# Another listed order for the engines of an attention-plus-MLP kernel: all that stands behind the first GEMM 1 product

## The chip, the cores and the metric

The kernel runs on one core of one Trainium2 chip. The metric is the device time of one execution in microseconds (us), lower is better. A core has a matrix engine (TensorE, PE in the profile, with its weight loads as PEld), a vector engine (VectorE, DVE), a scalar engine (ScalarE, ACT), a general engine (GpSimd, POOL) and a fifth one that only issues transfers (SyncE, SP). Each engine works through its own list of instructions in order; between engines there are semaphores.

## The reference

```python
# q, k, v: [4, 8, 768, 64] float32 (batch, head, position, width)
k_sum = k.reshape(B, H, nb, 32, D).max(axis=3)        # 24 blocks of 32 keys
v_sum = v.reshape(B, H, nb, 32, D).mean(axis=3)
scores_l = where(|i - j| < 16, scale * q @ k.T, -1e9)  # a narrow band
scores_s = scale * q @ k_sum.T + log(32)
a = softmax(concat([scores_l, scores_s]))
attn = a @ concat([v, v_sum])
x = attn as [3072, 512]
h = x @ w_in                                           # w_in [512, 2048]
out = (h * clip(h + 3, 0, 6) / 6) @ w_out              # w_out [2048, 512], out [3072, 512] float32
```

## The kernel before

The 3072 rows of x are worked on as eight tiles of 384 rows, two for each of the four batches. For every tile s there are 16 products of GEMM 1, named `F{s}x{ft}` (ft is the column block of 128 of w_in): four matmuls of 128x384 each, then `relu` on ACT (line 671) and `gate` on DVE (line 672), which together make the activation and write one slice of the buffer g. GEMM 2 is `G{s}{ts}x{a}`: three row groups ts for a tile, each with four parts of four matmuls of 128x512 (line 684); the last row group of the last tile is cut into pieces of 256, 128 and 128 columns (`G71x0`, `G71x256`, `G71x384`). A copy (`.4`) brings the sum from PSUM to a buffer `ot`, and a store (`.5`) writes it out.

Attention comes ahead of each pair of tiles. `K`, `Q`, `V`, `H` are loads of keys, queries and values, `w` the turning of keys and queries on DVE and ACT with the block maxima, `s` scores (small matmuls, then `exp` on ACT and masking on DVE), `u` the sums of values, `v` the products with the values (for the first four tiles with transposes `v....3` on PE), `h` copies of borders. `I0`, `I2`, `I4`, `I8`, `I12` load w_in: I0 its column blocks 0 and 1, I2 blocks 2 and 3, I4 blocks 4 to 7, I8 blocks 8 to 11, I12 blocks 12 to 15. `O0` to `O3` load w_out. All these loads are issued by POOL on one queue.

What sets the order on every engine is a table of names, `ORDER`. Each step of the kernel is recorded first with its engine, its inputs and the buffers that it touches (`Plan.op`), and `Plan.issue` then walks through the table and issues the steps in just that order. A name may end in `:A` or `:D`, which puts a copy on ACT or on DVE. Where a step needs a buffer out of a pool, it takes the one that has been free for longest, so another order also gives other buffers. The pools have three PSUM banks `h` and one `o`, two pairs of banks `S`, and four buffers `ot`.

```python
for n, token in enumerate(ORDER.split()):
    ...
    key, _, e = token.partition(":")
    o = named.pop(key)
    ...
        b.pool, b.slot = min(((p, s) for p in b.among for s in self.pools[p]), key=lambda x: since[id(x[1])])
    ...
    (partial(o.fn, {"A": "ACT", "D": "DVE", "P": "POOL"}[e]) if e else o.fn)()
```

A product of GEMM 1 waits for its own load of w_in, since it names the column block among its inputs, and the load names the blocks that it writes:

```python
op("POOL", "dma1024", lambda: nc.gpsimd.dma_start(out=w_in_sb[:, :, lo * 128:hi * 128], in_=w_in_v[:, :, lo * 128:hi * 128]),
   w=[("win", ft) for ft in range(lo, hi)], size=128 * (hi - lo))
...
op("PE", f"F{hi - lo}", lambda lo=lo, hi=hi: mms(lo, hi), r=[xt[s], ("win", ft)] + (xs if len(parts) == 1 else xs[lo:hi]), w=[h])
```

The first five products of tile 0 are issued as four separate steps (`F0x3.0` to `F0x3.3`) because x of that tile arrives in four pieces.

Of the kernel before, what the change touches and what calls it, by code (L numbers as in the profile page):

```python
# [15 lines left out]
D = 64  # L16
# [21 lines left out]
s001.2 F0x8.0 F0x8.1 F0x8.2 F0x5.1 I0.0 F0x5.2 F0x11.0 F0x1.0 F0x11.1 F0x11.2 F0x1.1 F0x1.2 F0x1.3 F0x1.4 F0x1.5 v410.0 v410.1  # L38
F0x7.0 F0x7.1 F0x7.2 v410.2 F0x10.0 F0x10.1 I12.0 F0x13.0 F0x13.1 F0x15.0 F0x15.1 F0x13.2 F0x10.2 v411.3 v411.4:D v410.3
v410.4:A F0x15.2 F0x14.0 F0x14.1 F0x14.2 F0x9.0 F0x9.1 F0x9.2 F0x0.0 F0x0.1 F0x2.0 F0x2.1 K13.0 K10.0 c.12:A F0x0.2 K12.0 K11.0  # L40
w10.0 Q1w1.0 F1x14.0 F1x14.1 F1x14.2 F1x4.0 F1x4.1 F1x4.2 F1x2.0 F1x2.1 F1x2.2 w10.1:D F0x2.2 F0x2.3 F0x2.4 F0x12.0 F0x12.1
F0x12.2 F1x8.0 F1x8.1 F1x8.2 F1x1.0 F1x1.1 F1x1.2 F0x0.3 F0x0.4 F0x0.5 F0x2.5 F1x9.0 F1x9.1 F1x9.2 F1x5.0 F1x5.1 F1x5.2 F1x15.0
F1x15.1 w11.0 w11.2 F1x15.2 w11.3:D Q1w4.0 Q1w2.0 Q1w0.0 w10.2 w10.3:D q6.0 q6.1:A q7.0 q7.1:A F1x7.0 F1x7.1 w11.1:A F1x7.2
F1x12.0 F1x12.1 F1x12.2 O0.0 G02x0.0 Q1w5.0 Q1w3.0 q4.0 q4.1:A q5.0 q5.1:A F1x6.0 F1x6.1 F1x6.2 O1.0 G02x0.1 s100.0 s100.1
s100.3 F1x3.0 w12.0 F1x11.0 F1x11.1 w13.0 w13.2 F1x3.1 F1x11.2 w12.2 w12.1:D O2.0 G02x0.2 s101.0 s101.1 O3.0 F1x10.0 G02x0.3
G02x0.4:A w13.3:D w13.1:A s101.3 F1x0.0 G00x0.0 G00x0.1 w12.3:D s100.2 s101.2 s100.4 V10.0 h100.0:D F1x10.1 h110.0:A F1x10.2
F1x3.2 s110.0 s110.1 s110.2 s101.4 s110.3 G00x0.2 G00x0.3 G00x0.4:A V12.0 u4.0 h130.0:D h120.0:A F1x0.1 u4.1:D u4.2:A u4.4:D
u4.3:D u4.5:D G02x0.5 G01x0.0 G01x0.1 G01x0.2 s110.4 F1x0.2 h111.0:A v100.0 v100.1 v100.2 h121.0:A v101.0 v101.1 v101.2 G01x0.3
G01x0.4:A K20.0 K21.0 K22.0 K30.0 K23.0 w21.0 F1x13.0 F1x13.1 F1x13.2 v100.3 v100.4:A w20.0 w21.3 G12x0.0 w21.2:A v101.3
v101.4:A V22.0 H2.0 h101.0:A w20.3 G12x0.1 G12x0.2 F2x2.0 F2x2.1 F2x11.0 F2x2.2 F2x11.1 F2x11.2 s111.0 w23.0 s111.3 F2x1.0  # L50
# [30 lines left out]
F7x6.2 G51x0.5 F7x8.0 F7x8.1 F7x8.2 G62x0.0 F7x4.0 F7x4.1 F7x4.2 F7x3.1 F7x3.2 F7x2.0 G62x0.1 F7x15.0 F7x2.1 F7x2.2 F7x15.1
F7x15.2 F7x0.0 G62x0.2 F7x0.1 G62x0.3 F7x7.0 F7x7.1 F7x0.2 G71x0.0 G62x0.4:D G62x0.5 F7x7.2 F7x11.0 F7x11.1 G61x0.0 F7x11.2
F7x14.0 G71x0.1 G71x0.2 G71x256.0 G61x0.1 F7x14.1 F7x14.2 G71x0.3 G71x0.4:A G72x0.0 G72x0.1 G71x0.5 G41x0.5 G70x0.0 G61x0.2
G61x0.3 G61x0.4:A G52x0.5 G70x0.1 G70x0.2 G72x0.2 G50x0.0 G50x0.1 G61x0.5 G50x0.2 G50x0.3 G72x0.3 G70x0.3 G50x0.4:A G50x0.5
G70x0.4:D G70x0.5 G60x0.0 G60x0.1 G60x0.2 G72x0.4:D G72x0.5 G60x0.3 G71x256.1 G71x256.2 G60x0.4:D G60x0.5 G71x256.3 G71x256.4
G71x384.0 G71x384.1 G71x384.2 G71x384.3 G71x384.4:D G71x384.5
"""


# [720 lines left out]
```

## Time and profile before

| | before |
|---|---|
| time, median of 3 runs | 217.0 us (216.62 to 217.43) |
| span of the profiled execution | 214.9 us |
| PE busy | 208.8 us (97%) |
| DVE busy | 162.7 us (76%) |
| ACT busy | 135.9 us (63%) |
| POOL busy | 49.5 us (23%) |

The profiled execution is shown by its span alone, from the first to the last instruction. The median is 2.1 us above that span, and this is taken as what lies around it. PE is close to always busy, so a microsecond in which PE has nothing to do is, from the first product of GEMM 1 on, a microsecond of the whole. Busy time of a matmul counts its passage through the array, so that matmuls overlap; the pace is read from the start of one group to the start of the next.

### The profile page before, as it was taken

The numbers are of one execution on the slowest core, as the hardware profiler recorded it, in microseconds if no ns is written. First come the engines' busy times: TensorE is split into PE (matmuls) and PEld (weight loads), VectorE is DVE, ScalarE is ACT, GpSimd is POOL, SyncE is SP. The second block draws the span as 40 slices with busy tenths as digits, with TensorE's granted clock in tenths as the row PEclk, the third lists the DMA queues.
The fourth block names the chain that finished last, engine by engine and source line by source line (L and its number), as shares of the span: only waits on it lengthen the run. The fifth ranks groups of instructions, "written<-read, shape, count | busy, mean of one in ns | idle before, by whom it ended". The sixth has DMA issues, their size and how long they took to land.

```text
span 214.9 us, 6125 instructions
## 1 busy us (share of the span) xinstructions
PE 208.8 (97%) x2564; PEld 119.7 (56%) x2564; DVE 162.7 (76%) x318; ACT 135.9 (63%) x264; POOL 49.5 (23%) x66
## 2 busy tenths in 40 slices
PE   7998999999999999999999999999999999999994
PEld 7566656555555565565555555555555555564443
DVE  6987999999899999898899889887865555550021
ACT  3987878887898988756578696566346355520110
POOL 7977358906643244000000000000000000000000
PEclk9999999999999999999999999999999999999999
DMA  5999999999999999930334234113314400113123
GB/s 75 159 155 189 203 188 170 190 203 162 206 160 187 181 135 151 108 146 11 38 37 143 28 37 110 49 21 39 70 19 81 78 0 3 49 49 122 52 80 139
DMA packets 91724, 22.68 MB, mean 106 GB/s; under 512 B 82224, under 2 KB 88752, under 8 KB 91696
## 3 DMA queue, kind: packets, MB, share of 16 engines
q0 software_dynamic: 62288, 14.41, 72.7%
q1 hardware_dynamic: 29264, 7.80, 15.4%
q8 instruction: 20, 0.33, 0.6%
q10 hardware_dynamic: 144, 0.07, 0.1%
q14 instruction: 8, 0.07, 0.1%
HBM read 28.82 MB, written 6.29 MB: 163 GB/s over the span
## 4 chain that ended last, share of the span: by engine, by line
PE 86%; POOL 5%; DMA 4%; DVE 1%; ACT 1%; issue 1%; POOLq 0%
PE h L667 38%; PE o L684 33%; PE h L684 5%; DMA qwide<-in_q_dram 4%; PE S L624 3%; PE S L513 3%; POOL vaug L344 2%; PE S L554 1%; ACT vaug L242 1%; POOL first L306 1%; PE S L637 1%; POOL qwide L326 1%; PE S L440 1%; PE S L667 1%; POOL first L313 1%; PE h L582 1%
## 5 line engine op out<-in xcount | busy, mean ns | idle before, releaser
L667 PE MATMUL h<-x,win 128*128 128x384 bf16 x500 | 91.1, 326 | 0.3 <-DVE g L672 0.3
L671 ACT ACTIVATE r<-h 128x384 f32<-128x384 f32 x125 | 58.7, 492 | 38.8 <-PE h L667 36.8
L672 DVE SCALAR_TENSOR_TENSOR g<-r,h 128x384 bf16<-128x384 f32 x125 | 65.7, 546 | 22.7 <-ACT r L671 20.1
L684 PE MATMUL o<-wout,g 128*128 128x512 bf16 x336 | 81.7, 379 | 0.0
L667 PEld LDWEIGHTS <-win 128*128 128x128 bf16 x512 | 48.7, 98 | 35.9 <-issue 0.5
L684 PEld LDWEIGHTS <-g 128*128 128x128 bf16 x416 | 38.7, 98 | 37.4 <-issue 0.3
L521 ACT ACTIVATE at<-S 120x768 bf16<-120x768 f32 x24 | 18.6, 811 | 5.5 <-PE S L513 5.4
L242 ACT COPY ot<-o 128x512 f32<-128x512 f32 x17 | 10.0, 586 | 15.4 <-PE o L684 14.2
L522 DVE TENSOR_TENSOR at<-at,mask 96x768 bf16<-96x768 bf16 x24 | 12.6, 549 | 2.0 <-ACT at L521 1.6
L606 DVE TENSOR_TENSOR xn<-S,rc 128x768 bf16<-128x768 f32 x14 | 13.3, 950 | 0.3
L242 DVE COPY ot<-h 128x512 f32<-128x512 f32 (+1 forms) x3 | 1.6, 555 | 14.3 <-PE h L684 14.3
L344 POOL DMA_DIRECT2D vaug<-in_v_dram x10 | 11.8, 1191 | 0.4 <-DMA first<-in_k_dram 0.2
L684 PE MATMUL h<-wout,g 128*128 128x128 bf16 (+2 forms) x80 | 11.4, 294 | 0.0
L468 DVE TENSOR_REDUCE red<-kaug 128x24 bf16<-128x768 bf16 x12 | 11.2, 942 | 0.1
L242 ACT COPY vaug<-vaug 32x640 bf16<-32x640 bf16 (+3 forms) x17 | 8.9, 574 | 0.8 <-DMA vaug<-in_v_dram 0.5
L242 ACT COPY vaug<-vs 24x1536 bf16<-24x1536 bf16 x6 | 8.8, 1468 | 0.6 <-DVE vs L242 0.5
L456 DVE STREAM_TRANSPOSE kaug<-kraw 128x768 bf16<-128x768 bf16 x8 | 8.1, 1020 | 0.3 <-PE S L513 0.3
L778 PE MATMUL o<-idle 128*128 128x64 bf16 (+2 forms) x70 | 7.0, 278 | 1.1 <-DVE idle L288 1.1
L334 POOL DMA_DIRECT2D kraw<-in_k_dram x8 | 5.9, 737 | 8.9 <-DVE kaug L456 7.3
L513 PEld LDWEIGHTS <-kaug 32*128 32x128 bf16 x576 | 5.3, 92 | 4.4 <-issue 3.6
L643 DVE STREAM_TRANSPOSE y<-xn 128x768 bf16<-128x768 bf16 x8 | 7.6, 964 | 0.2
L624 PEld LDWEIGHTS <-at 120*64 120x64 bf16 x336 | 6.2, 111 | 2.6 <-issue 1.5
(107 smaller groups left out, 183.6 us busy)
## 6 DMA issues: line engine op xcount, KB each, us to landing
out_dram<-ot SPq DMA_DIRECT2D x19, 256.0 KB, 2.3
vaug<-in_v_dram POOLq DMA_DIRECT2D x6, 384.0 KB, 13.1
wout<-in_moe_w_out_dram POOLq DMA_DIRECT2D x4, 512.0 KB, 9.9
win<-in_moe_w_in_dram POOLq DMA_DIRECT2D x3, 512.0 KB, 10.8
kraw<-in_k_dram POOLq DMA_DIRECT2D x8, 192.0 KB, 12.9
x<-y SPq DMA_DIRECT2D x64, 24.0 KB, 2.0
first<-in_k_dram POOLq DMA_DIRECT2D x6, 192.0 KB, 12.3
first<-in_q_dram POOLq DMA_DIRECT2D x6, 192.0 KB, 12.3
```

Source lines behind the costliest of these rows:

```text
L242: {"ACT": nc.scalar.copy, "DVE": nc.vector.tensor_copy, "POOL": nc.gpsimd.tensor_copy}[eng](o, i)
L344: op("POOL", "dma128", lambda: nc.gpsimd.dma_start(out=o[BLK:WIN, a:z, 0:D], in_=rows[:, a:z]), w=[("v", b % 2, c) for c in range(lo, hi)] ...
L468: op("DVE", "max", lambda: nc.vector.tensor_reduce(red.slot[:], w[:, :, BLK:WIN].rearrange("p t (n c) -> p t n c", n=2), axis=AX.X, op=ALU ...
L513: nc.tensor.matmul(X[g // 2].slot[:, g % 2, i * QB:(i + 1) * QB], kaug[2 * u + m][rows, t], qT[rows, 2 * u + m, t * QB:(t + 1) * QB], star ...
L521: op("ACT", "exp", lambda a=a, e=e: nc.scalar.activation(a, X[e].slot[0:KEYS, :, 0:HALF], AF.Exp, scale=scl), r=[X[e]], w=[("at", p, half)])
L522: op("DVE", "masking", lambda m=m: nc.vector.tensor_tensor(m, m, mask[:, low(half):low(half) + HQ].unsqueeze(1).to_broadcast([WIN, 2, HQ, ...
L606: nc.vector.tensor_tensor(o, src[..., 0:D], r.unsqueeze(len(r.shape)).to_broadcast(list(o.shape)), op=ALU.mult)
L624: nc.tensor.matmul(X.slot[64 * c:64 * c + 64, i, m:m + D + 1], a[:, t * QB:(t + 1) * QB], vaug[b % 2][0:KEYS, h, t, 0:D + 1], start=True, ...
L667: nc.tensor.matmul(bank(h)[:, 0:HALF], w_in_sb[:, kt, cols], xt[s].slot[:, kt], start=(kt == 0), stop=(kt == NP - 1))
L671: op("ACT", "relu", lambda: nc.scalar.activation(r.slot[:], bank(h)[:, 0:HALF], AF.Relu, bias=0.5, scale=1.0 / 6.0), r=[h], w=[r])
L672: op("DVE", "gate", lambda: nc.vector.scalar_tensor_tensor(gt[s].slot[:, ft], r.slot[:], 1.0, bank(h)[:, 0:HALF], op0=ALU.min, op1=ALU.mul ...
L684: nc.tensor.matmul(o.slot[:, a:z], gt[s].slot[:, ft, ts * 128:(ts + 1) * 128], w_out_sb[:, ft, a:z], start=(ft == 0), stop=(ft == NFT - 1))
```

## The change

The table `ORDER` has other rows from the place where the last scores of the first half batch (`s031.2`) are listed. The steps are the same 964 and what each computes is the same. Everything ahead of that place stays: loads of the first batch, its scores and first values. Some copies change between ACT and DVE with their suffix. No function is touched.

```diff
-v02.4 s021.1 s011.1 s021.2 v03.4 v03.5:D s011.2 v02.5:A s031.0 s031.1 s001.0 s031.2 I2.0 F0x3.0 F0x3.1 F0x3.2 F0x3.3 F0x3.4
-F0x3.5 I4.0 F0x6.0 F0x6.1 F0x6.2 F0x4.0 F0x4.1 F0x4.2 F0x4.3 v411.0 v411.1 F0x5.0 F0x4.4 F0x4.5 v411.2 s001.1 I8.0 u0.2:A
+v02.4 s021.1 s011.1 s021.2 v03.4 v03.5:D s011.2 v02.5:A s031.0 s031.1 s001.0 s031.2 I0.0 I8.0 I2.0 F0x3.0 F0x3.1 u0.2:D I12.0
+F0x3.2 F0x3.3 I4.0 K10.0 F0x6.0 F0x3.4 F0x1.0 K11.0 K13.0 F0x4.0 F0x4.1 F0x3.5 s001.1 F0x6.1 F0x1.1 F0x4.2 F0x4.3 F0x1.2 s001.2
...
```

Three places show what the table does to the engines' own lists.

The first place is POOL's list of loads, from the first load of w_in to the first loads of the second batch's keys and queries. The name in brackets is the semaphore lane whose last transfer must have landed before the load is issued on that lane; the load then reports on the same lane. Before:

```order
L374 DMA win_80<-in_moe_w_in_dram 128x4x256 [waits DMASW5_49]
L374 DMA win_80<-in_moe_w_in_dram 128x4x512 [waits DMASW6_49]
L374 DMA win_80<-in_moe_w_in_dram 128x4x512 [waits DMASW7_49]
L374 DMA win_80<-in_moe_w_in_dram 128x4x256 [waits DMASW0_49]
L374 DMA win_80<-in_moe_w_in_dram 128x4x512 [waits DMASW1_49]
L334 DMA kraw_70<-in_k_dram 32x24x128 [waits DMASW2_49]
```

These five are I2, I4, I8, I0 and I12. With the change the same rows of the same engine read:

```order
L374 DMA win_80<-in_moe_w_in_dram 128x4x256 [waits DMASW5_49]
L374 DMA win_80<-in_moe_w_in_dram 128x4x512 [waits DMASW6_49]
L374 DMA win_80<-in_moe_w_in_dram 128x4x256 [waits DMASW7_49]
L374 DMA win_80<-in_moe_w_in_dram 128x4x512 [waits DMASW0_49]
L374 DMA win_80<-in_moe_w_in_dram 128x4x512 [waits DMASW1_49]
L334 DMA kraw_70<-in_k_dram 32x24x128 [waits DMASW2_49]
```

Now they are I0, I8, I2, I12 and I4: I2 moved from the first place to the third, I4 from the second to the last, and the bytes of the five together are the same.

The second place is PE's list at the first products of GEMM 1, where each product's first weight load waits for the lane of its load of w_in. Before (the products are F0x3, F0x6, F0x4, then the values v411; rows that repeat are left out):

```order
L667 LDWEIGHTS win_80 [waits DMASW5_49]
L667 MATMUL h2_92<-x0_97,win_80 128x384 [waits DVE_49]
...
L667 LDWEIGHTS win_80 [waits DMASW6_49]
L667 MATMUL h1_91<-x0_97,win_80 128x384
...
L667 MATMUL h0_90<-x0_97,win_80 128x384
...
L624 MATMUL S0_88<-vaug0_76,at2_74 64x65 [waits Activation_49]
```

With the change (F0x3, F0x6, then F0x1 and F0x4 in turns, then F0x11):

```order
L667 LDWEIGHTS win_80 [waits DMASW7_49]
L667 MATMUL h2_92<-x0_97,win_80 128x384 [waits DVE_49]
...
L667 LDWEIGHTS win_80 [waits DMASW1_49]
L667 MATMUL h1_91<-x0_97,win_80 128x384
...
L667 LDWEIGHTS win_80 [waits DMASW5_49]
L667 MATMUL h0_90<-x0_97,win_80 128x384
L667 MATMUL S0_88<-x0_97,win_80 128x384 [waits Activation_49]
...
L667 LDWEIGHTS win_80 [waits DMASW6_49]
```

F0x3 and F0x6 are still the first two products, but the first now waits for the third load of w_in and the second for the fifth.

The third place is the end of ACT's list, which copies the last sums from PSUM and issues one store. Before:

```order
L242 COPY ot0_119<-h2_92 128x256
L242 COPY ot2_121<-o0_93 128x512
L242 COPY ot0_119<-o0_93 128x512
L698 COPY ot0_119<-h0_90 128x128
L699 DMA out_0_dram<-ot0_119 128x128
```

With the change:

```order
L242 COPY ot1_120<-h0_90 128x512
L242 COPY ot3_122<-h2_92 128x256
L242 COPY ot0_119<-h1_91 128x128
L242 COPY ot1_120<-h0_90 128x512
L242 COPY ot2_121<-o0_93 128x512
L698 COPY ot3_122<-h2_92 128x128
L699 DMA out_0_dram<-ot3_122 128x128
```

ACT now also makes the copies that DVE made last; the last products on PE were `G71x384` and are now `G71x256`, with `G60x0.3` (four matmuls of 512 columns) right ahead of them, and the last store of SP was the 128 columns of `G71x384` and is now the 512 columns of `G60x0`.

On PE, a product of GEMM 1 or 2 and a transpose of x use the whole 128x128 array, and the scores, values, sums and query transposes use part of it. Stretches of PE's list that use part of the array between two that use the whole number 23 before and 22 with the change: v411 and v410 now stand next to each other.

More of the change, by code (lines that the diff above doesn't have):

```diff
@@ L35 @@
 q3.1:D q2.0 u1.1:A u1.2:D s020.2 v02.0 v02.1 v02.2 s021.0 v02.3 s030.2 v03.0 v03.1 q2.1:A v03.2 s011.0 v03.3 v00.4 v00.5:D
-v02.4 s021.1 s011.1 s021.2 v03.4 v03.5:D s011.2 v02.5:A s031.0 s031.1 s001.0 s031.2 I2.0 F0x3.0 F0x3.1 F0x3.2 F0x3.3 F0x3.4
-F0x3.5 I4.0 F0x6.0 F0x6.1 F0x6.2 F0x4.0 F0x4.1 F0x4.2 F0x4.3 v411.0 v411.1 F0x5.0 F0x4.4 F0x4.5 v411.2 s001.1 I8.0 u0.2:A
-s001.2 F0x8.0 F0x8.1 F0x8.2 F0x5.1 I0.0 F0x5.2 F0x11.0 F0x1.0 F0x11.1 F0x11.2 F0x1.1 F0x1.2 F0x1.3 F0x1.4 F0x1.5 v410.0 v410.1
@@ L39 @@
[L39 to L42, printed above, removed]
@@ L47 @@
[L47 to L50, printed above, removed]
@@ L81 @@
[L81 to L84, printed above, removed]
@@ L85 @@
-G70x0.4:D G70x0.5 G60x0.0 G60x0.1 G60x0.2 G72x0.4:D G72x0.5 G60x0.3 G71x256.1 G71x256.2 G60x0.4:D G60x0.5 G71x256.3 G71x256.4
-G71x384.0 G71x384.1 G71x384.2 G71x384.3 G71x384.4:D G71x384.5
+v02.4 s021.1 s011.1 s021.2 v03.4 v03.5:D s011.2 v02.5:A s031.0 s031.1 s001.0 s031.2 I0.0 I8.0 I2.0 F0x3.0 F0x3.1 u0.2:D I12.0
+F0x3.2 F0x3.3 I4.0 K10.0 F0x6.0 F0x3.4 F0x1.0 K11.0 K13.0 F0x4.0 F0x4.1 F0x3.5 s001.1 F0x6.1 F0x1.1 F0x4.2 F0x4.3 F0x1.2 s001.2
+F0x6.2 F0x1.3 K12.0 F0x11.0 F0x4.4 F0x4.5 F0x1.4 F0x1.5 v411.0 v410.0 F0x8.0 F0x11.1 F0x8.1 v411.1 Q1w0.0 F0x5.0 F0x11.2 F0x7.0
@@ new lines @@
+v411.2 F0x8.2 v410.1 F0x5.1 F0x5.2 F0x7.1 F0x15.0 F0x7.2 F0x13.0 Q1w1.0 F0x10.0 F0x15.1 v410.2 F0x13.1 v411.3 v410.3 F0x13.2
+F0x15.2 F0x14.0 Q1w2.0 v410.4:D F0x9.0 F0x10.1 v411.4:A F0x14.1 F0x2.0 F0x9.1 O0.0 F0x10.2 F1x2.0 O1.0 F0x0.0 F0x0.1 F0x14.2
+F0x0.2 F0x0.3 F0x9.2 F1x2.1 F1x2.2 F1x4.0 F1x4.1 w10.0 F1x14.0 F0x12.0 F0x2.1 F1x14.1 F1x4.2 F0x2.2 F1x14.2 F0x12.1 Q1w5.0
+F0x2.3 F1x15.0 F1x5.0 F0x0.4 F0x2.4 F0x12.2 F1x15.1 F0x0.5 F1x7.0 F0x2.5 q7.0 q6.0 F1x5.1 q7.1:A Q1w3.0 F1x15.2 F1x5.2 F1x7.1
@@ new lines @@
+Q1w4.0 F1x9.0 w11.0 F1x9.1 F1x7.2 F1x9.2 F1x8.0 O2.0 G02x0.0 q6.1:D w11.1:A F1x8.1 w11.2 w10.2 F1x1.0 F1x3.0 F1x8.2 w10.3:D
+w10.1:A F1x3.1 O3.0 F1x1.1 F1x1.2 G02x0.1 w11.3:D q5.0 V10.0 q4.0 F1x11.0 V12.0 q4.1:A F1x6.0 q5.1:D F1x3.2 s100.0 K21.0
+F1x13.0 F1x11.1 s100.3 F1x11.2 s100.1 w12.0 F1x10.0 F1x6.1 F1x13.1 G02x0.2 c.12:A s101.0 s100.4 w12.2 F1x6.2 F1x13.2 G02x0.3
+K20.0 s101.3 G02x0.4:A w13.0 w12.3:D w13.2 w13.1:A s101.1 K22.0 s100.2 F1x12.0 F1x0.0 w12.1:A F1x10.1 h100.0:D K23.0 G00x0.0
+G00x0.1 w13.3:D s110.0 s110.3 s101.2 G00x0.2 s110.1 G00x0.3 u4.0 G00x0.4:A h120.0:D h121.0:A F1x0.1 h130.0:D G01x0.0 Q33.0
@@ new lines @@
+F6x13.1 G62x0.1 F7x7.2 F6x15.2 F7x5.0 F7x14.0 G51x0.5 F6x13.2 F7x5.1 G62x0.2 F7x5.2 G62x0.3 F7x14.1 F7x2.0 F7x8.0 F7x14.2
+F7x9.0 G62x0.4:D G61x0.0 F7x2.1 G61x0.1 F7x9.1 F7x9.2 F7x1.0 F7x2.2 G61x0.2 G52x0.5 F7x8.1 F7x8.2 G61x0.3 F7x1.1 F7x3.0 F7x1.2
+F7x4.0 G61x0.4:A F7x3.1 F7x4.1 G32x0.5 F7x3.2 G50x0.0 F7x11.0 G50x0.1 F7x0.0 G50x0.2 G61x0.5 F7x11.1 F7x11.2 F7x0.1 G50x0.3
+F7x0.2 F7x4.2 F7x15.0 G70x0.0 F7x13.0 G50x0.4:A G70x0.1 F7x13.1 G60x0.0 F7x13.2 G60x0.1 F7x15.1 G70x0.2 F7x15.2 G71x0.0 G70x0.3
@@ L87 @@
+G71x0.1 G71x384.0 G71x384.1 G70x0.4:A G62x0.5 G71x0.2 G72x0.0 G72x0.1 G60x0.2 G71x384.2 G71x0.3 G72x0.2 G71x0.4:A G71x384.3
+G70x0.5 G71x384.4:A G71x256.0 G72x0.3 G50x0.5 G72x0.4:A G71x0.5 G60x0.3 G71x256.1 G72x0.5 G71x256.2 G71x256.3 G60x0.4:A
+G71x256.4 G71x384.5 G60x0.5
 """
```

66 lines of the change are left out of this document (32 added, 34 removed).

## Prediction

> **What bounds the kernel now.** I read the page first (shares, clock, the chain that ended last), then PE's waits from the first product of GEMM 1 on, then the times at which the loads of w_in land, since the change shuffles those, and last the end of the program.
>
> ```profile
> PE 208.8 (97%) x2564; PEld 119.7 (56%) x2564; DVE 162.7 (76%) x318; ACT 135.9 (63%) x264; POOL 49.5 (23%) x66
> PEclk9999999999999999999999999999999999999999
> PE 86%; POOL 5%; DMA 4%; DVE 1%; ACT 1%; issue 1%; POOLq 0%
> ```
>
> PE is the bound: 97% busy, 86% of the chain, at full clock throughout. The next fence holds PE's waits between 24.5 and 212 us, and its busy time from the start of the second product, F0x6, to its last matmul.
>
> ```profile
> PE h L667 <- DVE g L672: 0.3, 1, 0.3
> 24.83:211.93 187.10, 186.66 (x2114) 1.00 0.82 99
> ```
>
> In 187.1 us PE shows 0.44 us of idle time. So an order can win little here by removing waits, and each new wait of PE counts in full, unless an old one goes.
>
> **The loads of w_in.** These are POOL's issues of I2, I4, I8, I0, I12 (start, duration), and for the same five, in the same order, size and us from issue to landing.
>
> ```profile
> 13.48 0.76 POOL L374 DMA_DIRECT2D win<-in_moe_w_in_dram  x1 [0.54 <-DMA vaug<-in_v_dram]
> 14.38 0.74 POOL L374 DMA_DIRECT2D win<-in_moe_w_in_dram  x1
> 15.53 0.74 POOL L374 DMA_DIRECT2D win<-in_moe_w_in_dram  x1 [0.41 <-DMA vaug<-in_v_dram]
> 16.77 0.74 POOL L374 DMA_DIRECT2D win<-in_moe_w_in_dram  x1 [0.51 <-DMA vaug<-in_v_dram]
> 17.50 0.75 POOL L374 DMA_DIRECT2D win<-in_moe_w_in_dram  x1
> ```
>
> ```profile
> win<-in_moe_w_in_dram POOLq DMA_DIRECT2D x1, 256.0 KB, 7.4
> win<-in_moe_w_in_dram POOLq DMA_DIRECT2D x1, 512.0 KB, 9.1
> win<-in_moe_w_in_dram POOLq DMA_DIRECT2D x1, 512.0 KB, 10.8
> win<-in_moe_w_in_dram POOLq DMA_DIRECT2D x1, 256.0 KB, 10.8
> win<-in_moe_w_in_dram POOLq DMA_DIRECT2D x1, 512.0 KB, 12.9
> ```
>
> Sums of the two give landings at 20.9, 23.5, 26.3, 27.6 and 30.4. They come in the order of issue: 2.6 to 2.9 us after the one ahead for 512 KB, 1.3 for 256 KB. The queue is in arrears and works in turn, so a load's place decides when it lands. POOL's later issues, which wait for these landings, confirm the last three:
>
> ```profile
> 26.66 0.88 POOL L326 DMA_DIRECT2D qraw<-in_q_dram  x1 [2.01 <-DMA win<-in_moe_w_in_dram]
> 27.88 0.87 POOL L326 DMA_DIRECT2D qraw<-in_q_dram  x1 [0.34 <-DMA win<-in_moe_w_in_dram]
> 30.66 0.54 POOL L325 DMA_DIRECT2D qraw<-in_q_dram  x1 [1.91 <-DMA win<-in_moe_w_in_dram]
> ```
>
> PE uses them just after they land. The next rows are PE's timeline there; the first row holds F0x3, F0x6 and F0x4.
>
> ```profile
> 24.17 2.12 PE L667 MATMUL h<-x,win 128*128 128x384 bf16 x12
> 26.23 0.57 PE L624 MATMUL S<-vaug,at 120*64 120x65 bf16 x24
> 26.73 2.12 PE L667 MATMUL h<-x,win 128*128 128x384 bf16 x12
> 28.69 0.81 PE L667 MATMUL S<-x,win 128*128 128x384 bf16 x4
> 29.93 2.80 PE L667 MATMUL h<-x,win 128*128 128x384 bf16 x16
> 24.83:30.43 5.60, 5.60 (x77) 1.00 1.49 196
> ```
>
> **The change part by part.** *First products of GEMM 1.* F0x3 needs I2, now third: 20.9 for I0 in the first place, plus 2.6 for I8, plus 1.3, is 24.7, instead of a start at 24.17. Its matmuls take 0.65 us (a third of 26.73 to 28.69), to 25.4. F0x6 needs I4, now fifth. The five loads hold the same bytes as before, so the fifth lands where the fifth landed: 17.50 + 12.9 = 30.4. PE works in order; behind F0x6's wait stand F0x1, F0x4 and F0x11, whose weights (but for F0x4's) are there by 23.5, and they can't pass. So PE stands from 25.4 to 30.4. Before, F0x6 began at 24.83, and the last row above shows that PE was busy through all of 24.83 to 30.43: none of that time was free. Everything from F0x6 on shifts by 30.4 - 24.8 = **+5.6 us**; F0x3's own half microsecond lies inside. Bounds by the fastest and the slowest pace of the rows: 20.9 + 3 x 2.6 + 1.3 = 30.0 (+5.2) and 20.9 + 3 x 2.9 + 1.3 = 30.9 (+6.1). ACT and DVE can't use the pause: their next relu and gate in the list are F0x6's. ACT has the exp of s001 and DVE its masking and one copy ahead of that, then both wait too.
>
> *Borders.* One border stretch goes, v411 and v410 stand together. The rows of the chain give its price (start, us):
>
> ```profile
> 29.50 0.50 PE S L624 x24
> 61.09 0.95 PE S L624 x48
> 68.69 2.06 PE h L667 x12
> 81.44 1.95 PE h L667 x12
> ```
>
> Twelve GEMM 1 matmuls take 2.06 behind a small product, 1.95 behind a large one: 0.11 for leaving a border. Two value products next to each other take 0.95, alone 2 x 0.50. One border less is 0.11 + 0.05 = **-0.2 us**. Transposes that now stand in pairs bring nothing, they use the whole array already.
>
> *Old waits.* At most the 0.44 us of PE idle time can go. The new list leaves more work of PE between the release of the bank o and its next use in tile 0 (G02 to G00: two GEMM 1 products now stand between instead of one) and between u4 and the first values that need it (four parts of GEMM 2 instead of three). I take **-0.3**, bounds 0 and -0.44.
>
> *Loads of later batches.* K, Q, V, H and w_out change places on POOL by one to four loads each. PE comes 5.6 us later while the queue does not wait for it up to V12, so they are earlier in relation to PE; I cost them at nothing. If that cover went (no pause), the price would be one place, 1 to 3 us of lateness, only where the margin is smaller.
>
> *Copies moved.* 20 copies go from ACT to DVE and 16 the other way; each is off PE's path while the buffer that it frees comes free in time. Cover: the F, G and scores between. Zero, with a rival below.
>
> *The end.* Before, PE's last matmul ends at 211.9, DVE copies 128 columns, SP stores 64 KB:
>
> ```profile
> 205.26 0.59 ACT L242 COPY ot<-o 128x512 f32<-128x512 f32 x1 [5.50 <-PE o L684]
> 211.11 0.27 ACT L698 COPY ot<-h 128x128 f32<-128x128 f32 x1 [5.26 <-PE h L684]
> 211.40 0.37 ACTq L699 DMA_DIRECT2D out_dram<-ot  x1
> 211.96 0.29 DVE L242 COPY ot<-h 128x128 f32<-128x128 f32 x1 [0.82 <-PE h L684]
> out_dram<-ot SPq DMA_DIRECT2D x2, 256.0 KB, 2.3
> out_dram<-ot ACTq DMA_DIRECT2D x1, 64.0 KB, 2.1
> out_dram<-ot SPq DMA_DIRECT2D x1, 64.0 KB, 1.6
> ```
>
> So the last landing is 211.96 + 0.29 + 1.6, 1.9 to 2.0 us behind PE's end. With the change ACT copies G60x0 (0.59) while PE does the three last parts of G71x256, whose 12 matmuls take about 0.67 (see the 128-column row further down: 1.7 us for 28), so ACT is free at about PE's end; then 0.27 for G71x256 and 2.1 for its store on ACT's queue: 2.4 behind PE's end. SP's store of 256 KB of G60x0 starts at PE's end and lands at 2.3. So **+0.5 us** (bounds 0.2 and 0.8, by the store rows of 2.1 to 2.4 us).
>
> Sum: 5.6 - 0.2 - 0.3 + 0.5 = +5.6. Against the profiled execution that is a span of 214.9 + 5.6 = 220.5; with the 2.1 us that lie between span and median, 222.6.
>
> **The rivals.**
>
> *The clock falls in the pause.* PE stands for about 5 us, longer than any wait that the trace before shows, which never lost the clock. Its own start shows a slow TensorE: the same 128x128 form at 3.3 to 4.3 us, and at the end.
>
> ```profile
> 1.13 3.71 PE L778 MATMUL o<-idle 128*128 128x64 bf16 x55 [1.13 <-DVE idle L288]
> L778 PE MATMUL o<-idle 128*128 128x128 bf16 x10 | 1.3, 312 | 0.0
> L684 PE MATMUL h<-wout,g 128*128 128x128 bf16 x28 | 1.7, 219 | 0.0
> ```
>
> 0.13 us each against 0.06, still so 3.2 us after the first matmul (1.13 to 4.3). If it happened again behind the pause, some 3.2 us would run at half pace: +1.6, so 224.2. It decides only if the pause comes close to 5 us. The Trainium skill, "TensorE: Matmul & The Clock Gate", in its section "HAM oscillation — how this bites in real kernels", says that an idle stretch over about 3.4 us brings the clock to half and that this is paid again after each such wait. No row here shows such a fall.
>
> *No pause: I4 lands in time.* If a load's time hung on its size alone and not on its place, I4 would land long before 25.4 and what is left is -0.2 - 0.3 + 0.5: 217.0, no change; with the end's lower bound 216.6. This is the case that ends on the other side. Against it: 512 KB took 9.1, 10.8 and 12.9 us by place. The Trainium skill, "DMA: Bandwidth & Descriptors", section "Anatomy of one DMA — SWDGE (gpsimd) path", fits about 2.0 us plus bytes over 436 GB/s, an estimate of 3.2 us for 512 KB, by which I4 would land at 20.7 and nothing would wait. The trace disagrees, with 12.9 for the last.
>
> *DVE becomes the bound later.* Between 40 and 70 us it is nearly full:
>
> ```profile
> 40.00:70.00 30.00, 29.66 (x517) 16.55 (x517) 28.39 (x52) 25.66 (x47) 14.46 (x17) 1.00 1.93 185
> L242 DVE COPY vaug<-vs 24x1536 bf16<-24x1536 bf16 x3 | 1.8, 592 | 0.1
> ```
>
> 1.6 us of 30 are free, and the change puts two query copies, three border copies, one spread and one transposed copy on DVE there, and takes a spread and a key copy off. At the spread's 0.59 us each, the five that are more come to 3.0 us, 1.4 more than is free. If PE lost all of that: 224.0. It decides only once the free 1.6 us are used up. Against it: the list also moves turns and maxima behind that stretch.
>
> **How the numbers follow.** The forecast (pause, clock held) has a chance of 0.55, 222.6, with a range of its own of 221.5 to 223.3 from the bounds above. Clock falls: 0.27, 224.2. DVE: 0.10, 224.0. No pause: 0.08, 216.6 to 217.0. The range 221.2 to 225.0 takes in the first three with their bounds (the clock's with the high pause, 224.2 + 0.5, and a little for what no row tells) and leaves out the last and the tails. A change below 0.5% (1.1 us; the three runs spread over 0.8) can't be told from none. Slower by more: 0.91; within: 0.06; faster: 0.03, if there is no pause and old waits go besides.
>
> **What would show it.** Right: PE's waits have a row of line 667 on the load of w_in of about 5 us, PE idle from 25.4 to 30.4; the five loads land at the same times as before; PE's busy stretch behind it ends 5 us later than 211.9; the last store lands 2.4 us behind PE's end. Clock: the PEclk row has a digit below 9 near 30 us, matmuls of F0x1 and F0x4 are longer. Wrong: I4 landing before 27 us, or PE with waits of more than 1 us in all behind 31 us.

## The result: 226.0 us, 4.1% slower than before

| | before | after |
|---|---|---|
| time, median of 6 runs each | 217.06 us (216.62 to 217.43) | 226.02 us (225.10 to 226.96) |
| ratio | 1 | 1.0414, 95% interval 1.0386 to 1.0442 |
| span of the profiled execution | 214.9 us | 225.2 us |

The direction was forecast, and where the time goes first. The size was not: 222.6 was said, with a range that ended at 225.0. From the page of after come PE's busy time, the clock row, and the shares of the chain that ended last:

```profile
PE 211.3 (94%) x2564; PEld 120.5 (54%) x2564; DVE 160.8 (71%) x322; ACT 132.7 (59%) x260; POOL 49.4 (22%) x66
PEclk9999958999999999999999999999999999999999
PE 78%; DMA 9%; DVE 5%; POOL 4%; issue 1%; ACT 1%; POOLq 0%
```

PE's share of the chain fell from 86% to 78%, transfers went from 4% to 9% and DVE from 1% to 5%. The clock row now has a 5 and an 8: two slices of 5.6 us near 30 us. PE's waits from the first product of GEMM 1 on, in after (total us, times, longest):

```profile
PE h L667 <- DMA win<-in_moe_w_in_dram: 5.5, 2, 5.2
PE S L624 <- DVE at L522: 0.8, 1, 0.8
PE S L624 <- DVE vaug L242: 0.5, 1, 0.5
PE S L513 <- DVE kaug L242: 0.3, 1, 0.3
```

The first row is the pause at F0x6 (5.2) and a short wait at F0x3 (0.3). The other three are new and no term of the prediction holds them: one masking and two kinds of copies by DVE, on which scores and values wait. The only wait that before had behind 24.5 us (0.3 us on a gate) is gone.

**The pause.** POOL's issues of w_in in after, and below them, from issue to landing, the 1st (256 KB), 2nd (512), 3rd (256), 4th (512), and the median of the 4th and 5th:

```profile
14.32 0.76 POOL L374 DMA_DIRECT2D win<-in_moe_w_in_dram  x1
15.29 0.74 POOL L374 DMA_DIRECT2D win<-in_moe_w_in_dram  x1 [0.21 <-issue]
16.56 0.74 POOL L374 DMA_DIRECT2D win<-in_moe_w_in_dram  x1 [0.53 <-DMA vaug<-in_v_dram]
17.82 1.48 POOL L374 DMA_DIRECT2D win<-in_moe_w_in_dram  x2 [0.52 <-DMA vaug<-in_v_dram]
```

```profile
win<-in_moe_w_in_dram POOLq DMA_DIRECT2D x1, 256.0 KB, 7.3
win<-in_moe_w_in_dram POOLq DMA_DIRECT2D x1, 512.0 KB, 8.7
win<-in_moe_w_in_dram POOLq DMA_DIRECT2D x1, 256.0 KB, 8.8
win<-in_moe_w_in_dram POOLq DMA_DIRECT2D x1, 512.0 KB, 10.1
win<-in_moe_w_in_dram POOLq DMA_DIRECT2D x2, 512.0 KB, 11.4
```

The sums are 21.6, 24.0, 25.4, 27.9 and, for I4 (issued at 18.56, 12.7 us since 10.1 and 12.7 have the median 11.4), 31.3. This execution's front runs 0.84 us later than that of before (the first of these issues is at 14.32, there at 13.48); take that off and the five land at 20.8, 23.2, 24.6, 27.1 and 30.5, where the prediction had 20.9, 23.5, 24.7, 27.6 and 30.4. The shift is no work of the change: in the thirteen traces of this study the first of these issues lies between 13.0 and 14.6 us, and a run further down whose list ahead of it is that of before has it at 14.39. PE's timeline there:

```profile
25.37 0.82 PE L667 MATMUL h<-x,win 128*128 128x384 bf16 x4 [0.33 <-DMA win<-in_moe_w_in_dram]
31.35 1.78 PE L667 MATMUL h<-x,win 128*128 128x384 bf16 x5 [5.15 <-DMA win<-in_moe_w_in_dram]
```

F0x6 starts at 31.35, or 30.51 without the shift: 5.7 us later than before (24.83).

**The clock.** Four stretches of 3.41 us from 25.32 on, and the whole from F0x6 to PE's last matmul. Behind the length stand the busy time of PE, PEld, DVE, ACT and POOL, each with its number of instructions; the last three figures are the granted clock, the mean share of the DMA engines and GB/s:

```profile
25.32:28.73 3.41, 0.82 (x4) 0.31 (x4) 2.35 (x5) 1.60 (x3) 1.41 (x2) 0.99 1.25 205
28.73:32.15 3.42, 0.80 (x3) 0.44 (x4) 0.00 (x0) 0.00 (x0) 0.87 (x2) 0.50 1.77 181
32.15:35.56 3.41, 3.41 (x13) 1.59 (x11) 0.82 (x2) 1.13 (x3) 3.21 (x5) 0.51 2.18 165
35.56:38.97 3.41, 3.41 (x65) 2.18 (x64) 2.96 (x7) 1.81 (x4) 3.41 (x5) 1.00 1.41 202
31.35:221.76 190.41, 188.80 (x2112) 104.93 (x2112) 138.29 (x256) 112.33 (x223) 28.85 (x32) 0.99 0.75 90
```

The clock is full up to 28.73, half for two stretches, and full again from 35.56. PE works at half pace from 31.35 to 35.56, 4.2 us, and so loses 2.1. One step of 3.41 us at half clock lowers the mean of 225 us by 0.0076. The six runs of after have means of 0.977 to 0.992, which by this estimate is one to three such steps; this one has two. From F0x6 to PE's end 190.4 us pass, 3.3 more than the 187.1 of before.

**The three late waits.** PE's timeline at the scores s110, then the four parts of GEMM 2 ahead of v101, and the values v101 and v100:

```profile
63.47 0.21 PE L513 MATMUL S<-qT,kaug 32*128 32x64 bf16 x4
63.94 0.51 PE L513 MATMUL S<-qT,kaug 32*128 32x64 bf16 x44 [0.26 <-DVE kaug L242]
67.00 3.63 PE L684 MATMUL o<-wout,g 128*128 128x512 bf16 x16
70.56 0.22 PE L624 MATMUL S<-vaug,at 120*64 120x65 bf16 x2
71.62 0.54 PE L624 MATMUL S<-vaug,at 120*64 120x65 bf16 x22 [0.84 <-DVE at L522]
72.64 0.57 PE L624 MATMUL S<-vaug,at 120*64 120x65 bf16 x24 [0.49 <-DVE vaug L242]
```

Idle time is 0.26, 0.84 and 0.49 us. By starts it is more, since the last matmul before a wait keeps the array busy into it: two matmuls of v101 that follow each other at some 0.05 us take 1.06 to the third. By starts the three cost 0.36, 0.96 and 0.59, 1.9 us in all. With the clock's 2.1 that is 4.0, against 3.3 more. The 0.7 between the two I put down to gains of the new list; it is a remainder and not a reading, close to the 0.5 that was forecast for the border and the old waits.

**The end.** The last rows of PE, ACT and ACT's queue, and the time to landing of ACT's store:

```profile
220.92 0.83 PE L684 MATMUL h<-wout,g 128*128 128x128 bf16 x12
221.79 0.27 ACT L698 COPY ot<-h 128x128 f32<-128x128 f32 x1
222.09 0.37 ACTq L699 DMA_DIRECT2D out_dram<-ot  x1
```

```profile
out_dram<-ot ACTq DMA_DIRECT2D x1, 64.0 KB, 2.1
```

The last landing is at 222.09 + 2.1 = 224.2, 2.4 us behind PE's end at 221.75, as forecast; before it was 1.9.

The sum for this execution: front 0.8, pause 5.7, clock 2.1, late waits 1.9, gains -0.7, end 0.5, together 10.3, which is 225.2 less 214.9 (the gains are the remainder, so the sum has to close). It is the longest of the six runs of after, 0.9 above their median; the front's 0.8 is not the change's, since no list differs there.

### The profile page after: what moved, and what is told of

Read it like the earlier page. It is cut to its first block, busy times and chain, and to the rows that moved or that the text cites. A ratio compares the mean times of both kernels' runs of the same rounds, so it can differ in the third digit from the quotient of the medians.

```text
span 225.2 us, 6129 instructions
## 1 busy us (share of the span) xinstructions
PE 211.3 (94%) x2564; PEld 120.5 (54%) x2564; DVE 160.8 (71%) x322; ACT 132.7 (59%) x260; POOL 49.4 (22%) x66
## 3 DMA queue, kind: packets, MB, share of 16 engines
q1 hardware_dynamic: 29264, 7.80, 14.6%
## 4 chain that ended last, share of the span: by engine, by line
PE 78%; DMA 9%; DVE 5%; POOL 4%; issue 1%; ACT 1%; POOLq 0%
PE h L667 35%; PE o L684 29%; DMA win<-in_moe_w_in_dram 6%; PE h L684 5%; DMA vaug<-in_v_dram 4%; PE S L624 3%; PE S L513 2%; DVE vaug L242 2%; POOL vaug L344 1%; PE S L667 1%; PE S L554 1%; DVE at L522 1%; POOL first L306 1%; PE S L637 1%; DVE g L672 1%
## 5 line engine op out<-in xcount | busy, mean ns | idle before, releaser
L667 PE MATMUL h<-x,win 128*128 128x384 bf16 x500 | 93.4, 330 | 5.5 <-DMA win<-in_moe_w_in_dram 5.5
L667 PEld LDWEIGHTS <-win 128*128 128x128 bf16 x512 | 49.2, 99 | 42.8 <-DMA win<-in_moe_w_in_dram 6.0
L521 ACT ACTIVATE at<-S 120x768 bf16<-120x768 f32 x24 | 18.9, 808 | 3.4 <-PE S L513 2.5
L242 ACT COPY ot<-o 128x512 f32<-128x512 f32 x20 | 11.7, 585 | 11.5 <-PE o L684 11.5
L684 PE MATMUL h<-wout,g 128*128 128x512 bf16 (+2 forms) x80 | 11.3, 294 | 0.0
L242 DVE COPY vaug<-vaug 32x768 bf16<-32x768 bf16 (+2 forms) x13 | 5.7, 469 | 4.5 <-PE S L554 2.8
L624 PE MATMUL S<-vaug,at 120*64 120x65 bf16 x336 | 7.1, 196 | 1.3 <-DVE at L522 0.8
L242 ACT COPY vaug<-vs 24x1536 bf16<-24x1536 bf16 x5 | 7.3, 1468 | 1.1 <-DVE vs L242 1.0
L496 ACT ACTIVATE at<-S 120x768 bf16<-120x768 f32 x8 | 6.4, 810 | 2.0 <-PE S L490 1.8
## 6 DMA issues: line engine op xcount, KB each, us to landing
vaug<-in_v_dram POOLq DMA_DIRECT2D x6, 384.0 KB, 10.1
win<-in_moe_w_in_dram POOLq DMA_DIRECT2D x3, 512.0 KB, 10.1
```

The source lines that it names most:

```text
L242: {"ACT": nc.scalar.copy, "DVE": nc.vector.tensor_copy, "POOL": nc.gpsimd.tensor_copy}[eng](o, i)
L521: op("ACT", "exp", lambda a=a, e=e: nc.scalar.activation(a, X[e].slot[0:KEYS, :, 0:HALF], AF.Exp, scale=scl), r=[X[e]], w=[("at", p, half)])
L624: nc.tensor.matmul(X.slot[64 * c:64 * c + 64, i, m:m + D + 1], a[:, t * QB:(t + 1) * QB], vaug[b % 2][0:KEYS, h, t, 0:D + 1], start=True, ...
L667: nc.tensor.matmul(bank(h)[:, 0:HALF], w_in_sb[:, kt, cols], xt[s].slot[:, kt], start=(kt == 0), stop=(kt == NP - 1))
L684: nc.tensor.matmul(o.slot[:, a:z], gt[s].slot[:, ft, ts * 128:(ts + 1) * 128], w_out_sb[:, ft, a:z], start=(ft == 0), stop=(ft == NFT - 1))
```

## The experiments

Ratios are to runs of before on the same chip. The first question was whether the pause and the clock are all.

**Loads of w_in in the order of use.** The new list, with the five loads sorted as PE needs them (I2, I4, I0, I8, I12):

```diff
-... s031.2 I0.0 I8.0 I2.0 F0x3.0 F0x3.1 u0.2:D I12.0 F0x3.2 F0x3.3 I4.0 K10.0 F0x6.0
+... s031.2 I2.0 I4.0 I0.0 F0x3.0 F0x3.1 u0.2:D I8.0 F0x3.2 F0x3.3 I12.0 K10.0 F0x6.0
```

> The changed kernel with the five loads of w_in issued in the order of their first use on PE (I2, I4, I0, I8, I12) and nothing else changed. Theory: the pause of 5.3 us before F0x6 goes and with it the half clock behind it (2.1 us), and the 0.5 us longer end and some 1.9 us of waits at s110, v101 and v100 stay: about 217.1 + 9.0 - 5.7 - 2.1 = 218.3 us, clock 1.0 throughout. Rival 1 (the new list is slow mainly by itself, the pause only hides it): above 220.5. Rival 2 (the waits at s110, v101, v100 come from the shift against the loads and go with the pause): 216.5 to 217.3.

Measured: 219.5 us (218.1 to 220.4), ratio 1.0114, interval 1.0068 to 1.0160. That is 2.6 us above before on its chip, so 6.3 of the 9.0 us are gone, and 1.2 us more are left than was expected. The three late waits stand as in after, with 0.3 us at s110, 0.7 at v101 and 0.5 at v100. So the order of the loads carries the pause and the fall of the clock behind it; the 2.6 us have other causes. They are known to 1 us only: the four executions lie 2.3 us apart. In the profiled one the clock fell for one step without a pause (told at the end), and two at full clock took 219.2 and 219.8.

**The pause without the fall.** The new list, with twenty products of no use (operands of the idle buffer) in the pause:

```diff
-F0x3.2 F0x3.3 I4.0 K10.0 F0x6.0
+F0x3.2 F0x3.3 ~20 I4.0 K10.0 F0x6.0
```

> The changed kernel with 20 idle matmuls of 512 columns (about 4.3 us of PE) put between F0x3 and F0x6, where PE stands and waits for I4. Theory: the pause stays, the clock does not fall, so only its 2.1 us go: about 224.0 us, PEclk 9 in every slice. Rival (the half clock is hidden behind DVE and ACT, which refill in that time): 225.5 to 226 with a clean clock row.

Measured: 224.1 us (223.4 to 224.4), ratio 1.0320, interval 1.0286 to 1.0353. Mean clock of the profiled execution, and the pause in PE's timeline:

```profile
core 0: 222.7 us, clock 0.997
```

```profile
25.64 4.48 PE L778 MATMUL o<-idle 128*128 128x512 bf16 x20
30.87 0.99 PE L667 MATMUL h<-x,win 128*128 128x384 bf16 x5 [0.75 <-DMA win<-in_moe_w_in_dram]
```

F0x6 still starts 5.9 us behind F0x3 (6.0 in after), the clock held, and 2.0 us are saved, as expected. That is the price of the fall, measured by itself.

**The pause in the kernel before.** Its list with the loads shuffled as in the change, nothing else:

```diff
-... I2.0 F0x3.0 ... I4.0 F0x6.0 ... I8.0 ... I0.0 ... I12.0
+... I0.0 I8.0 I2.0 F0x3.0 ... I12.0 ... I4.0 F0x6.0
```

> The kernel before with only the five loads of w_in in the changed order (I0, I8, I2, I12, I4). Theory: F0x6 waits for the fifth landing as in the changed kernel, 5.3 to 5.8 us, and the clock falls: 217.1 + 5.6 + 2.1 = 224.8 us. Rival (the pause needs the rest of the new list as well, or the list before makes up for it later): under 221 us.

Measured: 224.2 us (223.4 to 224.4), ratio 1.0330, interval 1.0303 to 1.0358, the clock fell here too (in this trace for one step, from 30.5 to 33.9, 2.9 us of it behind the pause), and PE's wait is much the same:

```profile
PE h L667 <- DMA win<-in_moe_w_in_dram: 5.1, 2, 4.7
```

Five rows of POOL's list, moved alone, make the kernel before 7.3 us slower. Everything else in the change adds 1.8 us on top (226.0 less 224.2).

**Two border copies on ACT.** What holds the DVE chain up? Two copies stood out in after, h100 at 62.48 and h130, the second of two at 67.11. Rows of DVE and of POOL at these places, and all border copies of DVE in after together (shortest/median/longest ns):

```profile
62.12 1.34 POOL L344 DMA_DIRECT2D vaug<-in_v_dram  x1
62.48 1.13 DVE L242 COPY vaug<-vaug 32x768 bf16<-32x768 bf16 x1
66.95 1.48 POOL L344 DMA_DIRECT2D vaug<-in_v_dram  x1
67.11 1.48 DVE L242 COPY vaug<-vaug 32x768 bf16<-32x768 bf16 x2 [2.77 <-PE S L554]
```

```profile
L242 DVE COPY vaug<-vaug x13: 170/349/1199, 14.0 to 73.5; 32x768 bf16<-32x768 bf16 x7, 32x640 bf16<-32x640 bf16 x3, 32x128 bf16<-32x128 bf16 x3
```

The usual copy takes 0.35 us (before, the longest was 0.49), these two took 1.13 and 1.20, and each ended 0.15 us behind the end of an issue of POOL. The edit puts both on ACT:

```diff
-h100.0:D ... h130.0:D
+h100.0:A ... h130.0:A
```

> The changed kernel with the two border copies h100 and h130 on ACT instead of DVE. In the trace of the changed kernel these took 1.13 and 1.20 us on DVE instead of 0.35, each while POOL issued a load of v (1.34 to 1.48 us). Theory: DVE's chain to s110, v101 and v100 gets shorter by 0.8 us twice and PE's waits there shrink from 1.9 to about 0.6: 226.0 - 1.3 = 224.7 us. Rival (the copies on ACT, about 0.83 us each, delay the spread on ACT by as much): 225.7 to 226.3.

Measured: 224.7 us (223.8 to 225.7), ratio 1.0359, interval 1.0319 to 1.0400. Of the three late waits one is left:

```profile
PE S L624 <- DVE vaug L242: 0.4, 1, 0.4
```

These two copies carry the waits at s110 and v101, 1.4 us, as expected. Whether it is the copies as such or POOL that lengthens them, this run doesn't tell.

**The chain and the end, on top of the sorted loads.** Three runs share this base: the chain alone, the end alone, and both.

```diff
 chain:
-h100.0:D ... h130.0:D ... u4.4:D u4.3:D s110.4 G01x0.3 F1x10.2 u4.2:D F1x0.2 v101.0
+h100.0:A ... h130.0:A ... u4.4:D s110.4 u4.3:D u4.2:D G01x0.3 F1x10.2 F1x0.2 v101.0
 end:
-... G60x0.3 G71x256.1 G72x0.5 G71x256.2 G71x256.3 G60x0.4:A G71x256.4 G71x384.5 G60x0.5
+... G60x0.3 G60x0.4:D G72x0.5 G71x256.0 G71x256.1 G71x256.2 G71x256.3 G71x256.4 G60x0.5 G71x384.2 G71x384.3 G71x384.4:D G71x384.5
```

> The changed kernel with the loads of w_in in the order of use (as in e1_loads_by_use) and, besides, the chain behind the border copies shortened: h100 and h130 on ACT, and on DVE the masking s110.4 ahead of the spreads u4.3 and u4.2 (so that v101 and v100 come a little later on PE's list than their inputs). Theory: what e1_loads_by_use (219.5) has left over before is 1.8 us of waits at s110, v101 and v100 and 0.5 us at the end; the first goes, 217.7 us. Rival: DVE is short of time as such, so that the waits turn up at a later product; then 219 us or more, with PE's waits on DVE still above 1 us between 60 and 80 us.

> The changed kernel with the loads of w_in in the order of use and, besides, the end as before the change: the parts of G71x384 are PE's last, DVE copies them and the last store is SP's 64 KB. Theory: 0.5 us of e1_loads_by_use's 219.5 go, 219.0 us, and the last landing is 1.9 us behind PE's end instead of 2.4. Rival: the end's length hangs on the order of the stores before it and not on who copies last; then 219.5 us.

> The two edits of e5 and e6 together, with the loads of w_in in the order of use. Theory (pause, clock, chain and end are all that the change cost): 217.2 us, level with before (216.9), or up to 0.5 us below it if the border and the old waits bring what the prediction gave them. Rival: there is a further cost spread over many products that no single wait shows; then 218 us or more.

Measured: chain 218.5 (218.2 to 218.8), ratio 1.0081, 1.0060 to 1.0102; end 217.8 (217.7 to 218.1), 1.0047, 1.0029 to 1.0064; both 217.7 (217.1 to 218.5), 1.0042, 1.0024 to 1.0061. None met its number. The chain alone brought 1.0 instead of 1.8, and its waits say why:

```profile
PE h L667 <- DMA win<-in_moe_w_in_dram: 0.5, 1, 0.5
PE o L684 <- DVE g L672: 0.5, 1, 0.5
PE S L624 <- DVE vaug L242: 0.4, 1, 0.4
```

s110 and v101 no longer wait, but v100 does, and two waits stand that after doesn't have. The sorted loads have one of their own: F0x11 needs I8, now fourth, and stands for 0.5 us. The other comes with this edit: the GEMM 2 product right behind v100 (at 64.42) waits 0.5 us for a gate of DVE, since both spreads now go ahead of the gates there. The end alone brought 1.7 instead of 0.5. 0.4 us is the end: the last landing is 2.0 us behind PE's end instead of 2.4. Another 0.8 came by luck, and it is the most telling reading of this study: nothing that the edit touches lies near v101, yet its wait is gone. In this run POOL issued V20 (59.60) only when h130 had begun (59.50); three copies took 0.89 us together, where in after two took 1.48:

```profile
59.23 0.89 DVE L242 COPY vaug<-vaug 32x768 bf16<-32x768 bf16 x3 [2.77 <-PE S L554]
59.60 1.48 POOL L344 DMA_DIRECT2D vaug<-in_v_dram  x1 [0.54 <-DMA first<-in_k_dram]
```

The rest, 0.5, lies within the spread of the base. With both edits 0.8 us above before are left, and the waits that are left explain them: F0x11 (0.4 by starts), v100 (0.5) and the GEMM 2 product behind it (0.6), less the 0.7 of gains.

**Does POOL lengthen the copies?** A first try moved the value load V22 behind Q20 in POOL's list and V20 up to the place right behind it, nothing else:

```diff
-V22.0 ... Q20.0 ... V20.0
+Q20.0 V22.0 V20.0
```

> The changed kernel with one edit: POOL issues the value loads V22 (two issues) and V20 one place later and one earlier, behind Q20, so that none is being issued while DVE makes the border copies h100 and h130 (at about 62.5 and 67.4 us). Nothing changes on PE, DVE or ACT. Theory (DVE's copy within SBUF stands still while POOL issues a value load): both copies take 0.35 us instead of 1.13 and 1.20, the wait at s110 (0.36 us) goes and that at v101 (0.96) falls to about 0.1, v100 keeps 0.6; 1.2 us less than the changed kernel, 224.8. Rival (the copies are long for a reason of their own, or DVE has too much to do there): they stay at 1.1 us and the time at 226.0.

Measured: 226.2 us (225.8 to 227.3), ratio 1.0441, interval 1.0413 to 1.0468; nothing gained, which is the rival's number. The rows show that the edit missed its aim: the second issue that I had put down to V22 belongs to H2, another load of values, which moved into the gap, and h100 ran into that one instead:

```profile
61.29 1.34 POOL L353 DMA_DIRECT2D vaug<-in_v_dram  x1
61.66 1.12 DVE L242 COPY vaug<-vaug 32x768 bf16<-32x768 bf16 x1
```

Again it ended 0.15 us behind POOL (62.63 and 62.78). The second try moves one load. K31 waits 5.4 us for a buffer, and all of POOL's list behind it; put behind Q20, it lets V22, H2 and Q20 go out during that wait:

```diff
-K31.0 ... V22.0 ... H2.0 ... Q20.0
+V22.0 ... H2.0 ... Q20.0 K31.0
```

> The changed kernel with one load moved: K31, which waits for DVE to release the key buffer (5.4 us in the changed kernel, until 61.3 us), is issued behind Q20 instead of ahead of V22, so the value loads V22 and H2 and the query load Q20 are issued during that wait, and POOL's later issues (V20, K30, Q21 among them) come some 4 us earlier. Lists of PE, DVE and ACT stay as they are. Theory (DVE's copies within SBUF are held while POOL issues a load): h100, h130 and the spreads u4.4, u4.3 and u4.2 meet at most one 0.7 us issue between them; the waits at s110, v101 and v100 (0.36, 0.96, 0.59) fall to 0.5 us in all; 1.4 us less than the changed kernel, 224.6. Rival (DVE simply has too much to do there): waits and time stay, 226.0.

Measured: 224.5 us (223.5 to 225.3), ratio 1.0333, interval 1.0306 to 1.0359. POOL's and DVE's rows at h100, the three border copies h120, h130 and h110, and what is left of the waits:

```profile
62.22 0.80 POOL L334 DMA_DIRECT2D first<-in_q_dram  x1
61.98 0.42 DVE L242 COPY vaug<-vaug 32x768 bf16<-32x768 bf16 x1
66.17 1.11 DVE L242 COPY vaug<-vaug 32x768 bf16<-32x768 bf16 x3 [3.04 <-PE S L554]
```

```profile
PE S L624 <- DVE vaug L242: 0.5, 1, 0.5
```

The lists of PE, DVE and ACT are those of after, row for row. h100 takes 0.42 instead of 1.13, the three copies 1.11 instead of 1.74, the wait at s110 is gone, that at v101 is 0.2 by starts instead of 0.96, and 1.5 us of the whole go (1.1 by the waits in this trace). So POOL's issues hold DVE's copies up: the copies are on the same engine in the same order, and nothing but the moments of POOL's loads was changed. v100 keeps its 0.59: that one is the list itself, which puts the spread u4.2 behind a masking and a gate.

**Is there anything to win?** All repairs together: sorted loads, the old end, K31 behind Q20, and F0x5 and F0x11 exchanged on PE.

```diff
-K12.0 F0x11.0 F0x4.4 ... F0x5.0
+K12.0 F0x5.0 F0x4.4 ... F0x11.0
```

> The changed kernel with the loads of w_in in the order of use, the end as before the change (both as in e6_use_order_end, 217.8), K31 issued behind Q20 as in e9_k31_later, and on PE F0x5 in the place of F0x11 and F0x11 in that of F0x5, since F0x11 waits 0.6 us there for the fourth load. Theory: of e6's 217.8 go 0.6 at F0x11, 0.4 at s110 and 0.6 at v100; 216.2, 0.3% faster than before (216.9). Rival: the waits turn up at other products, or the earlier issues meet other copies of DVE; then 217 us or more.

Measured: 217.3 us, ratio 1.0017, interval 1.0005 to 1.0029; 1.1 above the number expected, and within the rival's. F0x11 waits no more, but PE does again at v101 on the masking (0.4 us idle) and still at v100 (0.5). By starts these are 1.1 us; less the 0.7 of gains that is 0.4, and 0.3 was measured. The last run went after these two, with the masking ahead of a spread on DVE and the spread u4.2 on ACT:

```diff
-u4.4:D u4.3:D s110.4 G01x0.3 F1x10.2 u4.2:D F1x0.2 v101.0
+u4.4:D s110.4 u4.3:D u4.2:A G01x0.3 F1x10.2 F1x0.2 v101.0
```

> e10_all_repairs (217.3) with the masking s110.4 ahead of the spread u4.3 on DVE and the spread u4.2 on ACT, behind u4.5. What is left there is PE's waits of 0.5 us each at v101 (masking s110.4) and at v100 (spread u4.2). Theory: both go, 216.3 us, 0.3% below before (216.9). Rival: ACT, which then makes two spreads in a row, is late with the copy of G01's sums, and PE waits for the bank o instead; then 217.0 us or more.

Measured: 217.5 us, ratio 1.0026, interval 0.9997 to 1.0054. It missed because two spreads on ACT take 2.96 us, and v100 waits for ACT instead (0.4 us idle):

```profile
61.03 2.96 ACT L242 COPY vaug<-vs 24x1536 bf16<-24x1536 bf16 x2 [0.20 <-DVE vs L242]
```

No version beats before. With its faults mended the new order is level with it to some 0.2%; its fewer borders and old waits, worth 0.7 us by the balances above, are used up by the waits at the values of the second batch.

## Why the prediction was right in part

- *Order and time of landing, the pause.* Right. The queue works in turn, I4 landed as reckoned, and 5.7 us were measured where +5.6 stood. The experiment on the kernel before shows that this part alone is the larger one. The rival without a pause is out.
- *The clock.* Here the choice of the likeliest case failed. The prediction itself put the pause at 5.0 us (25.4 to 30.4), and wrote that the clock's fall "decides only if the pause comes close to 5 us": by its own number the condition was met, and it still got 0.27, because no row of before showed such a fall. It was also undersized: 3.2 us at half pace were taken from the start of the program, 4.2 were measured (2.1 us lost; 2.0 by the warmed pause).
- *"Copies moved. ... Zero, with a rival below."* This step failed. The cover was named ("the F, G and scores between") and not measured at the places where it is shortest. Between the sums u4 and the values v101 stand four parts of GEMM 2 on PE, 3.6 us (67.00 to 70.56). DVE has to do there, after the sums, three border copies, a masking, the copy of the sums out of PSUM, two spreads and another masking: 67.11 to 71.57, 4.5 us in after. No share of busy time over 30 us shows that. By starts v101 and v100 wait 0.96 and 0.59 us behind this chain, and s110 0.36 behind a shorter one with h100 in it, 1.9 in all. The prediction's own sign of being wrong, more than 1 us of waits behind 31 us, came true. And the trace of before had the warning: there the chain that ended last leaves PE between the same sums and values and runs over ACT's copies for them, the second of which ends at 61.04, when PE starts on the values at 61.09. Nothing was to spare at this place:

```profile
58.34 0.82 ACT vaug L242
59.56 1.48 ACT vaug L242
```

- *DVE as the bound, the rival.* Half right in mechanism, wrong in place: DVE wasn't full. It stood idle for 2.8 us right ahead of the late chain (the 2.77 in the row at 67.11), waiting for PE's sums. What counts is the latency of a chain, not the free time of an engine.
- *Loads of later batches at nothing.* PE doesn't wait for them, as was said. But the price came another way: their issues on POOL held DVE's copies up, 1.1 us of the 1.9 by the waits of the trace with K31 moved, 1.5 by the times.
- *Border and old waits, -0.5.* The gain is there: -0.7 by the balance above. It was not tested apart; the same 0.7 closes the sums of the runs with both edits and with all repairs.
- *The end, +0.5.* Right to a tenth, 2.4 us behind PE's end.
- *Slower, 0.91.* Right. The sum with the terms as measured (pause 5.7, clock 2.1, waits 1.9, gains -0.7, end 0.5) is 9.5; 8.96 was the difference of the medians. Most of the half microsecond is the profiled execution of before, which lay 0.4 below its median: in all runs that list both, the time is 1.7 to 1.8 above the span, not 2.1.
- *The ranges.* The forecast's own range, 221.5 to 223.3, doesn't come out of its bounds: the lowest terms add up to 221.8 and the highest to 223.7. The clock's 2.1 and the chain's 1.9 together are what took the time past 225.0; either alone would not have.

## What to carry to other kernels

When an order moves loads on a queue that is in arrears, count the landing by place and then ask for each pause it makes whether the clock holds; if the forecast pause meets the rival's own condition, the rival is the forecast. Don't price moved copies by an engine's free share: take each place where PE consumes them, and set the time PE has for other work since the last input against the sum of the steps of the chain. And a load that moves can cost time where nobody waits for its data, by the moment at which it is issued.

## What the runs showed of the hardware that was not expected

**A copy of DVE stands still while POOL issues a transfer.** Seven times a 32x768 copy, 0.35 us by itself, ended 0.15 to 0.18 us behind the end of a POOL issue: two in after (1.13 and 1.20 us), three with the value loads moved (1.12, 0.66 and 0.57), two with K31 moved (0.42 and 0.58). The other ten traces hold twelve more that ended by the same margin. In the three traces named, five copies that began within 0.16 us of the issue's start were not held (one is the first of the two at 67.11, with POOL from 66.95 on). The gates and maskings don't get longer beside such issues (0.50 to 0.56 us in after, with and without). Before shows it as well, just ahead of the only wait of PE there (0.3 us on a gate): two copies of keys that take 0.25 and 0.16 us elsewhere took 1.19 together, until POOL's first issue was done.

```profile
38.21 2.69 POOL L344 DMA_DIRECT2D vaug<-in_v_dram  x2
38.51 1.19 DVE L242 COPY kaug<-kaug 128x352 bf16<-128x352 bf16 x2
```

The Trainium skill, "SBUF — State Buffer", section "Who interferes with whom", says that VectorE in its two-port modes and GpSimd share one pair of ports, that whoever comes first has it for a whole instruction, and that the other waits. The trace agrees in that a copy that comes later waits out POOL's issue; the five that began just behind its start and went on don't fit "the whole instruction". That it is the port, and not something else of POOL's, no run here shows.

**The clock falls and rises in steps of 3.41 us.** In after it fell at 28.73, 2.5 us after PE had stopped, and stayed low for two such steps, so more of the slow time lay behind the pause than in it. In the kernel before with the loads shuffled it fell at 30.5, 4.2 us after PE had stopped, and for one step. The Trainium skill, "TensorE: Matmul & The Clock Gate", section "HAM oscillation — how this bites in real kernels", tells of the fall after an idle stretch of more than about 3.4 us. This case agrees in that both pauses, 5.2 and 4.7 us, are longer than that and the clock fell; but in after it fell when PE had idled 2.5 us, at the end of a step in which PE had still worked 0.82 us (the row of 25.32 above).

**It can fall without any pause.** In the profiled execution with only the loads sorted, one step in the front was at half clock, while PE was busy in all of it:

```profile
24.36:27.77 3.41, 3.41 (x34) 1.81 (x31) 2.71 (x7) 2.30 (x5) 1.25 (x2) 0.50 1.25 207
```

In the step ahead of it PE did the small products of the front, which are the same in before. A run of before beside these experiments has the same mean clock, 0.992, and took 218.2 us where the median was 216.9. What sets this off is open; it was not tried.
